# A linear-attention and feed-forward kernel on one core: a step order from priorities replaced by a written-out order

## The chip, the cores and the metric

The kernel runs on one core of one Trainium2 chip. A core has TensorE (PE in the profile; its weight loads are PEld), VectorE (DVE), ScalarE (ACT), GpSimd (POOL), SyncE (SP, which here only issues DMAs) and 16 DMA engines. Each engine works through its own instructions in the order in which the program gave them, and waits at an instruction until what that one needs is there. The metric is the device time of one launch in microseconds (us).

## What is computed

The first half is a linear attention with decay (batch 4, 8 heads, 768 positions, head width 48), the second a feed-forward layer:

```python
for t in range(S):
    cur = np.einsum('bhd,bhe->bhde', u[None] * kt, vt)
    y[:, :, t] = np.einsum('bhd,bhde->bhe', rt, state + cur)
    state = wt[:, :, :, None] * state + np.einsum('bhd,bhe->bhde', kt, vt)
x = y.transpose(0, 2, 1, 3).reshape(B * S, H * D)   # 3072 x 384
h = x @ w_in                                        # 384 x 2048
out = np.maximum(0.01 * h, h) @ w_out               # 2048 x 384
```

All inputs and the output are float32; the matmuls run in bf16.

## The kernel before

**Tiles.** The sequence is cut into 24 chunks of 128 positions (6 per batch). The first two chunks of batches 0 and 1 are done as two pairs (`pair`, chunks 0/1 and 2/3); the others one by one (`single`, chunks 4 to 23, in turn over the batches). Each chunk goes through the same steps:

- SP loads w, k, r and v into a tile `in` (L630 for pairs, L845).
- ACT takes the logarithm of w (L644, L855). TensorE sums it cumulatively with a triangular matrix (L654, L861) and in total (L668, L864). DVE forms `ci` (L873); ACT takes the exponentials (L687, L882, L887, L891).
- DVE multiplies them into r and k (`rk`, L545). Transposing gives `rkT`: by TensorE (L556) with a copy on ACT (L563) or DVE (L561), or, for the chunks in `RK_DMA`, by a transposing DMA (L908).
- POOL casts v (`vb`, L595) and, with a row of `u` spread at the start (L528, L522, L533, L539: `ub`), makes products (`ru`, L575 and L579), which DVE sums (`dg`, L583) and POOL multiplies into v (`vs`, L587).
- TensorE makes the scores (L768, L1002), DVE masks them (`m`, L780, L932). TensorE makes the state's sums (L727, L942), DVE adds the old state (L957), and for the next chunk of the batch POOL scales the state (`sb`, L919; in the pairs DVE, L738).
- TensorE makes y from masked scores, v and state (L793, L800, L812; L968, L973); DVE or ACT takes it out of PSUM (L618; L822, L824). It is transposed into `xT` by TensorE (L604) with a copy (L609, L611), or by a DMA (L987).

**Feed-forward.** The chunks are put together to 15 blocks of one or two. Per block, TensorE makes the up-projection in steps of 512 columns of PSUM (L1168: 6 matmuls of 256 columns, or 12 of 128), ACT applies the leaky ReLU into `g` (L1183), TensorE makes the down-projection in four quarters of four matmuls per chunk (L1198), DVE or ACT copies it (L1209, L1211), SP stores it (L1215). In the last three blocks (`seven`) the down-projection is a scheme with seven products in place of eight (L1098), with sums on DVE (L1048 once for the weights, in `mix`; L1079 for each block; L1119). The weights are loaded at the start in pieces (L466, L471) and cast to bf16 on POOL, DVE or ACT (L488, L490, L492).

**What sets the order.** `Plan` holds 1092 steps. A step has the engines that could do it with a time for each, a function that issues its instructions, a priority, the steps that it depends on, the buffers that it reads and takes, and for a DMA a time on the wire. `Plan.order` (L43) plays this through in time: an engine that comes free takes, of the steps whose inputs are done and whose buffers are free, the one with the lowest priority. `RANK` (L163) shifts the priority of each step by a number, and `FORCE` (L301) ties some steps to one engine. What comes out is the program's order on every engine, and which buffer of its pool each step gets. Limits per kind of PSUM buffer (L450) and a slack (L344) enter too. In the first 24 us of the plan's own time, TensorE gets filler matmuls on zeros (L1240) in its gaps.

A PSUM bank is written and read by several steps, by different engines; the program orders their accesses to one tile in the order in which they are issued.

Of the kernel before, what the change touches and what calls it, by code (L numbers as in the profile page):

```python
# [15 lines left out]
class Buf:  # L16


    def __init__(self, pool, kind=None, wide=1):
        self.wide = wide  # L20
        self.pool, self.kind, self.users, self.t, self.free_at = pool, kind or pool, [], None, 0.0


class Plan:


    ENGINES = ("PE", "DVE", "ACT", "POOL", "SP")
# [4 lines left out]
    def __init__(self, limits, slack_from, slack, late):  # L32
        self.steps, self.limits, self.late = [], limits, late
        self.slack_from, self.slack = slack_from, slack
# [8 lines left out]
    def order(self, pools):  # L43
        n = len(self.steps)
        users = [[] for _ in range(n)]
        left = [len(s[3]) for s in self.steps]
        for i, s in enumerate(self.steps):
            for j in s[3]:
                users[j].append(i)
        bufs = {}  # L50
        for i, s in enumerate(self.steps):
            for b in (*s[4], *s[5]):
                bufs[id(b)] = b
        remain = {k: len(b.users) for k, b in bufs.items()}
        free_tiles = {p: [(0.0, k) for k in range(len(t))] for p, t in pools.items()}
        in_use = {}
        ready_at = [0.0] * n
        self.start, self.done, self.eng = [None] * n, [0.0] * n, [None] * n
        free = dict(self.BEGIN)
        ready = {e: [] for e in self.ENGINES}  # L60
        events = []
        dma_free, flying = 0.0, []

        def offer(i, t):
            for e in self.steps[i][0]:
                heapq.heappush(events, (t, 0, e, i))

        for i in range(n):
            if not left[i]:
                offer(i, 0.0)  # L70
        for e in self.ENGINES:
            heapq.heappush(events, (free[e], 1, e, -1))
        count, out = 0, []
        while events:
            now, kind, e, i = heapq.heappop(events)
            same = {e}
            if kind == 0 and self.start[i] is None:
                heapq.heappush(ready[e], (self.steps[i][2], i))
            elif kind == 2:
                in_use[i] -= 1  # L80
            while events and events[0][0] <= now + 1e-9:
                _, kind, e, i = heapq.heappop(events)
                same.add(e)
                if kind == 0 and self.start[i] is None:
                    heapq.heappush(ready[e], (self.steps[i][2], i))
                elif kind == 2:
                    in_use[i] -= 1
            for e in self.ENGINES:
                if (e not in same and "*" not in same) or free[e] > now + 1e-9:
                    continue  # L90
                held, chosen = [], None
                while ready[e]:
                    pri, i = heapq.heappop(ready[e])
                    if self.start[i] is not None:
                        continue
                    want, ok = {}, True
                    for b in self.steps[i][5]:
                        if b.t is None:
                            want[b.pool] = want.get(b.pool, 0) + 1
                            if in_use.get(b.kind, 0) >= self.limits.get(b.kind, 99):  # L100
                                ok = False
                    for p, k in want.items():
                        if sum(f <= now + 1e-9 for f, _ in free_tiles[p]) < k:
                            ok = False
                    if ok:
                        chosen = i
                        break
                    held.append((pri, i))
                for h in held:
                    heapq.heappush(ready[e], h)  # L110
                if chosen is None:
                    continue
                i = chosen
                engs, fn, pri, deps, reads, takes, wire = self.steps[i]
                for b in takes:
                    if b.t is None:
                        slots = free_tiles[b.pool]
                        s = min(slots)
                        slots.remove(s)
                        b.slot = s[1]  # L120
                        b.t = pools[b.pool][s[1]]
                        in_use[b.kind] = in_use.get(b.kind, 0) + 1
                d = engs[e]
                self.start[i], self.eng[i] = now, e
                out.append(i)
                count += 1
                free[e] = now + d - (self.OVER[e] if d > 0.3 else 0.0)
                if wire is None:
                    self.done[i] = now + d + self.SEEN[e]
                    if self.slack_from <= pri < 1000:  # L130
# [1144 lines left out]
```

## Time and profile before

| | |
|---|---|
| median of 3 runs | 178.79 us (178.79 to 179.43) |
| span of the profiled execution | 177.7 us |
| TensorE busy | 170.7 us, 2106 matmuls |
| DVE, ACT, POOL busy | 133.9, 115.6, 105.3 us |
| DMA moved | 34.24 MB in 115884 packets |

The profiled execution's own time is known by its span alone, from its first to its last instruction; the median of the runs, which also hold what lies around the span, is 1.1 us above it. Busy times of TensorE are modelled: its matmuls overlap, and a busy TensorE is not one at its peak. So what its work costs is read from the chain of waits, which gives for each piece the time from its start to that of the next.

### The profile page before, as it was taken

How to read it: one execution, taken by the hardware profiler on the slowest of the kernel's cores; microseconds unless marked ns; L12 is line 12 of the kernel's file. 1: busy time of each engine (PE TensorE's matmuls, PEld its weight loads, DVE VectorE, ACT ScalarE, POOL GpSimd, SP SyncE). 2: the span in 40 equal slices, each digit the busy share in tenths (PEclk: the TensorE clock that was granted, in tenths of full speed). 3: DMA queues.
4: the chain of work that ended last, by engine and by line, in shares of the span. 5: the costliest groups of instructions: out<-in, count | busy, mean ns of one | idle time of the engine just before them, and what ended most of it. 6: DMA issues, size and time to landing. Idle time of an engine off the chain costs nothing.

```text
span 177.7 us, 5379 instructions
## 1 busy us (share of the span) xinstructions
PE 170.7 (96%) x2106; PEld 133.9 (75%) x2110; DVE 133.9 (75%) x268; ACT 115.6 (65%) x258; POOL 105.3 (59%) x139
## 2 busy tenths in 40 slices
PE   7899899999999999999999999999999999999993
PEld 2456678766879767797788776788777798899992
DVE  7599744568987949979968888699779688776463
ACT  5679877764856687487497891288873677662820
POOL 5998554255897749993905994659884099100000
PEclk9999999999999999999999999999999999999999
DMA  5999999999999999997999999997999996613004
GB/s 142 262 283 341 338 377 325 234 197 168 193 146 210 171 189 191 194 227 171 221 185 209 197 147 222 205 177 155 191 208 148 241 207 160 159 24 111 4 22 157
DMA packets 115884, 34.24 MB, mean 193 GB/s; under 512 B 108305, under 2 KB 115090, under 8 KB 115858
## 3 DMA queue, kind: packets, MB, share of 16 engines
q1 hardware_dynamic: 115856, 33.89, 94.3%
q8 instruction: 16, 0.26, 0.7%
q14 instruction: 10, 0.08, 0.2%
q10 hardware_dynamic: 2, 0.00, 0.0%
HBM read 25.17 MB, written 4.72 MB: 168 GB/s over the span
## 4 chain that ended last, share of the span: by engine, by line
PE 74%; DMA 8%; SPq 5%; ACT 4%; DVE 3%; issue 3%; POOL 1%; DVEq 0%; ACTq 0%; POOLq 0%
PE ps L1168 29%; PE ps L1198 23%; PE ps L1098 8%; DMA in<-in_moe_w_in_dram 5%; SPq L630 4%; DMA in<-in_w_dram 3%; PE ps L1002 3%; PE ps L973 2%; ACT g L1183 2%; PE ps L861 2%; PE ps L556 2%; PE ps L968 2%; PE ps L942 1%; PE ps L604 1%; DVE in L1048 1%
## 5 line engine op out<-in xcount | busy, mean ns | idle before, releaser
L1168 PE MATMUL ps<-xT,w_in_b 128*128 128x256 bf16 (+1 forms) x720 | 73.3, 251 | 0.1
L1183 ACT ACTIVATE g<-ps 128x512 bf16<-128x512 f32 x96 | 55.9, 594 | 22.4 <-PE ps L1168 19.5
L1168 PEld LDWEIGHTS <-w_in_b 128*128 128x128 bf16 x720 | 57.6, 98 | 8.4 <-issue 0.3
L1198 PE MATMUL ps<-w_out_b,g 128*128 128x384 bf16 x288 | 56.5, 326 | 0.0
L1198 PEld LDWEIGHTS <-g 128*128 128x128 bf16 x288 | 25.1, 97 | 12.0
L545 DVE TENSOR_TENSOR rk<-in,ps 128x384 bf16<-128x384 f32 x48 | 25.3, 550 | 8.0 <-ACT ps L887 3.0
L575 POOL TENSOR_TENSOR ru<-in,ub 128x384 f32<-128x384 f32 x24 | 25.4, 1061 | 6.2 <-DMA in<-in_k_dram 6.1
L932 DVE TENSOR_TENSOR m<-ps,maskb 128x512 bf16<-128x512 f32 x40 | 25.3, 682 | 4.2 <-PE ps L1002 3.3
L595 POOL CAST vb<-in 128x384 bf16<-128x384 f32 x24 | 13.2, 553 | 22.3 <-DMA in<-in_v_dram 19.1
L579 POOL TENSOR_TENSOR ru<-ru,in 128x384 f32<-128x384 f32 x24 | 24.4, 1028 | 2.9 <-DMA in<-in_r_dram 2.4
L587 POOL TENSOR_TENSOR vs<-in,dg 128x384 f32<-128x384 f32 x20 | 17.0, 852 | 3.5 <-DVE dg L583 2.9
L919 POOL TENSOR_TENSOR sb<-s,a 128x384 bf16<-128x384 f32 x18 | 14.9, 830 | 3.3 <-ACT a L882 3.3
L873 DVE TENSOR_TENSOR ci<-ps,lw 128x384 f32<-128x384 f32 x20 | 11.1, 553 | 4.5 <-PE ps L861 1.8
L618 DVE TENSOR_TENSOR y<-ps,vs 128x384 bf16<-128x384 f32 x20 | 10.9, 553 | 4.5 <-PE ps L973 4.5
L583 DVE TENSOR_REDUCE dg<-ru 128x8 f32<-128x384 f32 x24 | 13.1, 544 | 0.7 <-POOL ru L579 0.6
L882 ACT ACTIVATE a<-ps 64x4 f32<-64x4 f32 x36 | 6.1, 168 | 11.6 <-DVE ci L873 8.9
L855 ACT ACTIVATE lw<-in 128x384 bf16<-128x384 f32 x20 | 10.1, 520 | 3.8 <-DMA in<-in_w_dram 3.6
L891 ACT ACTIVATE ps<-ci 128x384 f32<-128x384 f32 x20 | 9.7, 485 | 1.8 <-DVE ci L873 1.8
L887 ACT ACTIVATE ps<-ps 128x384 f32<-128x384 f32 x20 | 9.3, 467 | 0.5 <-DVE ci L873 0.3
L1240 PE MATMUL ps<-zeros 128*128 128x128 bf16 (+1 forms) x31 | 7.6, 351 | 1.6 <-DVE zeros L409 1.3
L556 PE MATMUL ps<-ident,rk 128*128 128x128 bf16 x88 | 8.4, 220 | 0.5 <-DVE rk L545 0.4
L1098 PEld LDWEIGHTS <-g 128*128 128x128 bf16 x96 | 8.1, 98 | 0.2
(105 smaller groups left out, 222.5 us busy)
## 6 DMA issues: line engine op xcount, KB each, us to landing
out_dram<-o SPq DMA_DIRECT2D x23, 192.0 KB, 2.7
in<-in_w_dram SPq DMA_DIRECT2D x20, 192.0 KB, 4.6
in<-in_v_dram SPq DMA_DIRECT2D x20, 192.0 KB, 4.9
in<-in_r_dram SPq DMA_DIRECT2D x20, 192.0 KB, 4.4
in<-in_k_dram SPq DMA_DIRECT2D x20, 192.0 KB, 4.6
in<-in_moe_w_out_dram SPq DMA_DIRECT2D x4, 768.0 KB, 8.7
in<-in_moe_w_in_dram SPq DMA_DIRECT2D x4, 384.0 KB, 7.8
in<-in_moe_w_in_dram SPq DMA_DIRECT2D x2, 768.0 KB, 8.5
```

The costliest lines, as they stand in the source:

```text
L545: (nc.gpsimd if e == "POOL" else nc.vector).tensor_tensor(out=o, in0=x, in1=i, op=ALU.mult)
L575: lambda e: nc.gpsimd.tensor_tensor(out=ru.t[:], in0=kv(), in1=ubv, op=ALU.mult),
L579: lambda e: nc.gpsimd.tensor_tensor(out=ru.t[:], in0=ru.t[:], in1=rv(), op=ALU.mult),
L583: lambda e: nc.vector.tensor_reduce(out=dg.t[:], in_=ru.t[:], axis=AX.X, op=ALU.add),
L587: lambda e: nc.gpsimd.tensor_tensor(out=vs.t[:], in0=vv(), in1=dg.t[:].unsqueeze(2).to_broadcast([128, H, D]), op=ALU.mult),
L595: {"POOL": 0.56}, lambda e: nc.gpsimd.tensor_copy(out=vb.t[:], in_=vv()),
L919: lambda e: nc.gpsimd.tensor_tensor(out=sb.t[:].rearrange("p g a d -> p (g a) d"), in0=s_in.t[:].rearrange("p g a d -> p (g a) d"), in1=a_ ...
L932: lambda e, par=par: nc.vector.tensor_tensor(out=m.t[:, par, :, :], in0=sc[par].t[:].rearrange("p (g t) -> p g t", g=NP), in1=maskb[:].uns ...
L1098: nc.tensor.matmul(o(), lhsT=x()[:, i, :], rhs=y()[:, i, :], start=fresh, stop=(stop and i == ii[-1]), skip_group_check=True)
L1168: nc.tensor.matmul(hp.t[:, a * N : (a + 1) * N], lhsT=w_in_b[:, t, (j + a) * 128 : (j + a + 1) * 128], rhs=xT[:, t, c0 : c0 + N], start=(a ...
L1183: lambda e, hp=hp, g=g, j=j, J=J, N=N: nc.scalar.activation(out=g.t[:, j : j + J, 0:N], in_=hp.t[:, 0 : J * N].rearrange("p (a n) -> p a n ...
L1198: nc.tensor.matmul(op.t[:, 0:DM], lhsT=g.t[:, j, off : off + 128], rhs=w_out_b[:, j, :], start=(j == 0), stop=(j == NJ - 1))
```

## The change

The steps and what each computes stay. Changed are:

- `Plan.order` no longer chooses. It goes through a list `ORDER` of all 1092 steps, and gives each engine its steps in that order. A step runs on the engine that `FORCE` names, or on the first one that its `add` call lists. The plan's times are kept, for buffers and for the filler matmuls; a PSUM buffer touched by one engine now counts as in use for the others until that access is done, and DMAs land in order.
- `RANK`, the limits per kind and the slack go. `FORCE` is a new table. By both, 43 steps run on another engine than before: among them the first copy of u's row (L528) from ACT to DVE, y's copies of the first pair (L822, L824) both to ACT and those of the second both to DVE, six of the copies out of transposes (L563) to DVE and five (L561) to ACT, and some weight casts.
- Several step times in the plan are set anew: casts of weights 0.57 on DVE (from 1.0 and 0.66), 0.95 for L1048 (from 1.2), 0.72 for a spaced copy of transposes, 0.68 for masks.
- Buffers: `in` 11 (from 10), `ci` 3 (from 2), `g` 4 (from 3), and the pairs' `rkT2` now takes a `g` buffer. `xT`, one tile for all chunks, becomes six buffers of one block each.
- The filler matmuls end at a step of the list (`warm_end`) as well as at 24 us.

The order itself, where the prediction speaks of it:

- SP, start: w, k, r of the first pair, w of the second, then v of the first (before: v, then w), k and r of the second, weight piece 4, piece 0, v of the second, pieces 1, 3, 2. Before: piece 0 stood ahead of k, and pieces 4 and 2 ahead of v.
- TensorE, first pair: L668 stands behind two of the transposes L556 (before: ahead of all). DVE: L738 behind all four masks L780 (before: between two and two). Up-projection steps of block 0: those of piece 4 first, three of the six ahead of L727 of the second pair, as before.
- SP, later: the w loads of chunks 8, 9, 11 and 13 stand earlier, many v loads later; the v loads of chunks 22 and 23 stand behind their transposing loads L908 (before: ahead).
- TensorE, later: the state sums L942 of chunks 6, 8, 9, 10, 11, 14 and 15 stand later; cumulative sums L861 of most chunks earlier. The last product steps and DVE's last five steps stand as before.
- The four L1048 stand further apart: two together, one, one (before: two together, then one and one with a step or two between).

```diff
     def order(self, pools):
...
+        for i in ORDER:
+            engs, fn, deps, reads, takes, wire = self.steps[i][0], *self.steps[i][1:2], *self.steps[i][3:]
+            if left[i]:
+                raise RuntimeError(("before its inputs", i))
+            e = FORCE.get(i) or next(iter(engs))
+            now = max(at[e], ready[i])
+            for b in takes:
+                if b.t is None:
+                    slot = min(free[b.pool])
+                    free[b.pool].remove(slot)
+                    now, b.slot, b.t = max(now, slot[0]), slot[1], pools[b.pool][slot[1]]
+            touched = list({id(b): b for b in (*reads, *takes)}.values())
+            for b in touched:
+                if b.pool == "ps":
+                    now = max([now, *(t for q, t in b.seen.items() if q != e)])
+            self.start[i], self.eng[i] = now, e
+            at[e] = now + engs[e] - (self.OVER[e] if engs[e] > 0.3 else 0.0)
...
+                landed = self.done[i] = max(wire_free + lat, landed + 0.7 * time)
...
-RANK = {0: -309.63, 1: -310.62, 2: -303.35, 3: -175.12, 4: -176.12, 5: -3.85, 6: -313.07, 7: -303.34, 8:
...
+ORDER = [1090, 0, 1, 2, 3, 4, 5, 6, 7, 11, 14, 12, 13, 20, 18, 19, 21, 8, 25, 26, 27, 36, 22, 23, 40, 24, 15,
...
-    xT = pool.tile([128, KT, NCH * L], BF16, name="xT")
-
-    make("in", 10, [128, 1536], F32)
+
+    make("in", 11, [128, 1536], F32)
...
-    make("ci", 2, [128, H, D], F32)
+    make("ci", 3, [128, H, D], F32)
...
-    make("rkT2", 2, [128, 2 * NP, 256], BF16)
...
-    make("g", 3, [128, NJ, max(blocks) * L], BF16)
+    make("g", 4, [128, NJ, max(blocks) * L], BF16)
+    make("xT", 6, [128, KT, max(blocks) * L], BF16)
...
+        place = {}
+        for nb, size in enumerate(blocks):
+            xb = Buf("xT")
+            for off in range(size):
+                place[len(place)] = (xb, off * L)
...
-            rkT = Buf("rkT2")
+            rkT = Buf("g", "rkT2")
...
-                    {"DVE": 1.2}, sub, MIX_RANK, deps=[*wout_s, last], reads=t[: x // 2 + 1], takes=[t[x // 2]])
+                    {"DVE": 0.95}, sub, MIX_RANK, deps=[*wout_s, last], reads=t[: x // 2 + 1], takes=[t[x // 2]])
```

214 lines of the change are left out of this document (67 added, 147 removed), and 188 rows, old and new, of tables (ORDER, RANK).

## The prediction

> **What bounds the kernel now.** I read the page first: busy shares, the slices and the DMA queue.
>
> ```profile
> span 177.7 us, 5379 instructions
> ...
> PE 170.7 (96%) x2106; PEld 133.9 (75%) x2110; DVE 133.9 (75%) x268; ACT 115.6 (65%) x258; POOL 105.3 (59%) x139
> ...
> PEclk9999999999999999999999999999999999999999
> DMA  5999999999999999997999999997999996613004
> GB/s 142 262 283 341 338 377 325 234 197 168 193 146 210 171 189 191 194 227 171 221 185 209 197 147 222 205 177 155 191 208 148 241 207 160 159 24 111 4 22 157
> DMA packets 115884, 34.24 MB, mean 193 GB/s; under 512 B 108305, under 2 KB 115090, under 8 KB 115858
> ...
> q1 hardware_dynamic: 115856, 33.89, 94.3%
> ```
>
> Two resources are near their limit: TensorE, at full clock in every slice, and the DMA engines, busy until some 150 us (slice 34 of 40). The other three engines have room, so moving a step between DVE, ACT and POOL changes the time only by when its result is there.
>
> Next, the chain of waits (start, us, what), for what TensorE's work costs when nothing holds it up.
>
> ```profile
> 26.05 1.34 PE ps L1168 x24
> 36.13 1.30 PE ps L1198 x8
> 80.96 0.55 PE ps L1002 x16
> 116.20 0.17 PE ps L968 x4
> 116.37 0.20 PE ps L973 x8
> 144.57 3.28 PE ps L1168 x30
> 168.78 5.95 PE ps L1098 x72
> 174.76 0.36 DVE o L1119
> ```
>
> Per step: an up-projection step of a one-chunk block (12 matmuls of 128 columns) takes 0.67, one of a two-chunk block (6 of 256) 3.28/5 = 0.656, a quarter of a down-projection 0.65, an L1098 matmul 0.083. From 26.05 on TensorE has 24 x 0.67 + 66 x 0.656 (all but the first six) + 72 x 0.65 + 168 x 0.083 = 120.1 us of these; scores about 5.8 (seven of 0.55, six near 0.33), the y steps 20 x 0.37 = 7.4, and some 254 small matmuls near 0.05 (transposes, cumulative sums, state sums) 13. That is about 146.5 us. The last matmul ends at 168.78 + 5.95 = 174.7, so the stretch from 26.05 lasts 148.7. **Only about 2.2 us are lost there; the other loss is the first 26 us**, in which TensorE does the two pairs' matmuls and six up steps, an estimated 15 us. A new order can gain in just these two places; behind 174.7 come a 0.36 us addition and a store, 3.0 us, which the change leaves alone.
>
> **The change part by part.** The steps, and the work in each, stay; so does the sum of TensorE's work. New are the order on each engine, the engine of 43 steps, and buffers. I go by stretches of the span.
>
> *The first 26 us.* The timeline there:
>
> ```profile
> 3.18 0.51 ACT L528 COPY o<-o 1x384 f32<-1x384 f32 x1
> 4.84 0.50 PE L533 MATMUL ps<-o,ones_f 128*128 128x384 bf16 x1 [0.20 <-DVE o L522]
> 7.00 1.02 DVE L545 TENSOR_TENSOR rk<-in,ps 128x384 bf16<-128x384 f32 x2 [1.06 <-PE ps L668]
> 11.06 1.29 DVE L780 TENSOR_TENSOR m<-ps,mask 128x512 bf16<-128x512 f32 x2 [0.17 <-PE ps L768]
> 12.27 0.55 DVE L738 TENSOR_TENSOR sb<-ps,a 128x384 bf16<-128x384 f32 x1
> 12.74 1.28 DVE L780 TENSOR_TENSOR m<-ps,mask 128x512 bf16<-128x512 f32 x2
> 14.06 0.57 PE L793 MATMUL ps<-vb,m 64*128 64x48 bf16 x32
> 16.07 0.48 ACT L824 CAST y<-ps 128x384 bf16<-128x384 f32 x1
> 16.10 0.56 DVE L822 CAST y<-ps 128x384 bf16<-128x384 f32 x1 [0.16 <-PE ps L812]
> 18.20 0.81 PE L1168 MATMUL ps<-xT,w_in_b 128*128 128x256 bf16 x6
> 20.68 0.96 POOL L595 CAST vb<-in 128x384 bf16<-128x384 f32 x2 [1.80 <-DMA in<-in_v_dram]
> 21.24 0.22 PE L727 MATMUL ps<-vb,rk 64*128 64x96 bf16 x2 [0.43 <-POOL vb L595]
> ```
>
> - The first row of u (L528, 0.51) goes from ACT to the end of DVE's row of L522, so L533 starts near 5.3 instead of 4.84. The cumulative matmuls waited for the logarithms anyway; I take 0.1 (0 to 0.5). ub, and POOL's chain of products behind it, come 0.3 later, which POOL's row hides until the reductions L583 that stand ahead of the masks on DVE.
> - L668 goes behind two transposes. DVE's first product waited 1.06 and named L668; without it it can start near 6.6 instead of 7.00: -0.4.
> - L738 goes behind all four masks instead of between them: the last mask, and with it L793, come up to 0.55 earlier, near 13.45 instead of 14.06.
> - The pair's two L824 copies and the two xT copies now all stand on ACT, with an L563 copy between them, where before ACT and DVE shared them (16.07 and 16.10). That is 2 x 0.48 on the path, and the 0.6 gained is given back: the first up-projection starts near 18.5 instead of 18.20, +0.3.
> - SP now issues the second w ahead of the first v, and one 384 KB weight load that stood ahead of the second pair's v goes behind it. At the page's 338 GB/s in that slice, 393 KB is an estimated 1.2 us: v, for which POOL waited 1.80, comes near 19.5, and L727 starts behind three up-projections near 20.6 instead of waiting up to 21.24. What follows up to the first step of block 1 is the same list of steps.
>
> Together the row at 26.05 moves to about 25.2: **-0.9**, from -1.6 (v 1.8 earlier and no series on ACT) to +0.8 (ACT's series costs its full length, v is no earlier).
>
> *From there to the last chunks.* The two largest stalls, by the chain, and the DVE rows beside the second:
>
> ```profile
> 55.41 6.14 DMA in<-in_w_dram
> 61.57 0.52 ACT lw L855
> ...
> 66.35 0.33 PE ps L942 x4
> ...
> 127.88 0.42 ACT lw L855
> ...
> 128.35 0.32 PE ps L861
> ```
>
> ```profile
> L1048 DVE TENSOR_TENSOR in<-w_out_b x2: 1236/1494/1751, 118.2 to 119.3; 128x1536 bf16<-128x1536 bf16 x2
> ```
>
> ```profile
> 159.59 0.69 DVE L1079 TENSOR_TENSOR in<-g 128x1024 bf16<-128x1024 bf16 x1 [0.73 <-ACT g L1183]
> ```
>
> The first is a late w load: the logarithm, the sums and the exponentials behind it end in L942, for which TensorE waits half a microsecond. In the new order the w loads of chunks 8 and 9 stand five and nine places earlier in SP's row and that L942 step 22 places later in TensorE's, so this wait goes. The second is ACT's logarithm at 127.88, behind products that DVE did late because of four subtractions L1048. They ran beside POOL steps and took 1.24 to 1.75; L1079, of the same kind and with POOL at rest, took 0.69 for 1024 columns, so 1536 should take near 1.03. Spread out and kept apart from POOL, the four give back up to 4 x 0.45 = 1.8 us of DVE. What is late next: the state sums L942 of five chunks go 17 to 28 us later in TensorE's work, and the state update, POOL's scaling and the next chunk's y now follow with little between (the one of chunk 6 has some 2.2 us of TensorE steps before chunk 10's y, for a path of 0.17 + 0.55 + 0.83 and the hand-overs). I take half of the loss, **-1.1**, from -2.2 (all of it) to +2 (several new waits of half a microsecond).
>
> [...]
>
> *Buffers.* An eleventh load buffer lets SP run ahead of the chunks; a third ci, a fourth g and six xT blocks remove waits that no row shows to be on the chain: 0. The shared g and rkT2 cost nothing as long as the pairs are done before the fourth block, which the order has.
>
> *The end.* The last products and DVE's last five steps stand as before: 0.
>
> **How the DMA limits this.** SP's rows and chunk 22, the last one computed:
>
> ```profile
> in<-in_v_dram SPq DMA_DIRECT2D x20, 192.0 KB, 4.9
> ```
>
> ```profile
> 141.92 2.08 SPq L845 DMA_DIRECT2D in<-in_v_dram  x2
> 147.27 0.50 POOL L595 CAST vb<-in 128x384 bf16<-128x384 f32 x1
> 147.69 0.33 PE L861 MATMUL ps<-lw,trev 128*128 128x384 bf16 x1
> 151.13 1.29 SPq L908 DMA_TRANSPOSE rkT<-rk  x1
> 157.73 0.33 PE L968 MATMUL ps<-sb,rkT 128*128 128x96 bf16 x4
> ```
>
> Behind the start of chunk 22's y (157.73) the new order leaves TensorE ten up steps, 136 L1098 matmuls and the y itself: 6.6 + 11.3 + 0.4 = 18.2 us; before, 17.0 passed to the end. So to end by 172.7, 2 us earlier, that y must come at 154.5. Its k and r loads keep their places. The transposing load at 151.13 waited for a cumulative sum that came late in TensorE's row (147.69) and now stands twelve places earlier there. Issued by 148, with both v loads now behind it (1.3 for itself, about 1.5 for what follows, 3 to 4.9 to land), v is there at 153.8 to 155.7 and y half a microsecond later. This is about the -2 of the sum, and it is why I don't take the whole -3.1.
>
> **The sum.** 177.7 - 0.9 - 1.1 = 175.7 of span. The profile gives no more of its own execution than the span; the median of the runs, 178.79, lies 1.1 above it, which I carry over: **176.8 us**.
>
> **Rivals.**
>
> *The DMA sets the pace all the same.* For: 94.3% and nines in every slice to 150; the bytes stay; chunks' y steps stand 1 to 6 us earlier in TensorE's work than they ran, so TensorE may merely wait for them. Against: only y's of late loads matter, and stores and far-ahead loads were moved behind. Then 157.73 stays and the time is 178.3 to 179.4. [...]
>
> *A head-of-line wait in SP's queue: slower.* Chunk 22's and 23's v loads were issued at 141.92; now they stand behind the transposing loads of both chunks, and those behind DVE's products. If the last of these is issued no earlier than before (151.13), v is issued near 153.9 and lands at 156.9 to 158.8, and y comes at 157.6 to 159.5 with 18.2 behind it: 1 to 3 us later than now, 179.9 to 181.8. It decides from an issue at about 149.5 on.
>
> *The new order doesn't do what it says:* the first 26 us get longer by 0.8 and the new state waits eat the rest: 178.8 to 180.
>
> **How the numbers follow.** A measurement of this kernel tells about 0.5% from no change: 177.9 to 179.7 is "the same". Forecast 0.55 (175.2 to 177.9), the whole gain and more 0.07 (under 175.2), the DMA's pace 0.16, SP's queue 0.12, the order itself 0.10, half of it slower. So faster 0.62, same 0.21, slower 0.17. The range 175.0 to 180.3 leaves out about 0.05 below and 0.1 above.
>
> **What would show it.** Right: the first step of block 1 near 25.2; L727 without a wait for vb; L1048 near 1.0; no L942 on the chain at 66; chunk 22's y at 153.5 to 156; the last matmul near 172.7. Wrong: transposing loads of chunks 22 and 23 issued after 149.5, POOL's cast of v waiting just ahead of the last y, a first up-projection past 19, or TensorE idle in the middle slices with ACT or DVE named. The prediction fails in its sum if the first 26 us don't shorten, since more than half of the rest rests on waits that I only know in the old order.

## The result and the profile after

The changed kernel takes 180.02 us (median of 20 runs, 178.91 to 181.97), the kernel before 179.23 (20 runs, 178.77 to 179.57). The ratio is **1.0032 [1.0019, 1.0045]**: a third of a per cent slower. In a later set of runs it was 1.0046 [1.0022, 1.0071]. One of the changed kernel's 20 executions in the first set (181.97, at a granted clock of 0.991) fell into a slower state and is left out of the ratio. The profiled execution took 180.19; its span is 178.5, 0.8 longer than before, and the forecast was 175.7.

The changed kernel's code is shorter, so that the same step has a line number some 140 lower: the up-projection L1168 is L1028 now, the down-projection L1198 is L1058, the cumulative sum L861 is L722, the logarithm L855 is L716, the scores L1002 are L862, the loads L845 are L706. In the experiments the numbers differ a little again.

The page of the changed kernel, the lines that answer to those shown of before:

```profile
span 178.5 us, 5374 instructions
...
PE 169.7 (95%) x2103; PEld 133.9 (75%) x2106; DVE 132.6 (74%) x275; ACT 111.9 (63%) x249; POOL 105.1 (59%) x141
...
PEclk9999999999999999999999999999999999999999
DMA  5999999998999999999999999996998938721113
...
q1 hardware_dynamic: 115856, 33.89, 94.8%
q8 instruction: 16, 0.26, 0.6%
```

Work, clock and bytes are those of before; what changed is waiting. So I compare the two traces step by step: for each TensorE step the time from its start to the next one's, above what steps of its kind take at their shortest. Three differences make up the span.

**The first 26 us: -1.1, as forecast.** The timeline of the changed kernel (start, us, engine, line, operation; in brackets the wait ahead of it):

```profile
5.32 0.34 PE L393 MATMUL ps<-o,ones_f 128*128 128x384 bf16 x1 [0.47 <-DVE o L388]
...
6.65 1.95 DVE L405 TENSOR_TENSOR rk<-in,ps 128x384 bf16<-128x384 f32 x4 [0.39 <-ACT ps L549]
...
18.08 2.21 PE L1028 MATMUL ps<-xT,w_in_b 128*128 128x256 bf16 x18
...
20.45 0.52 PE L589 MATMUL ps<-vb,rk 64*128 64x96 bf16 x16 [0.16 <-POOL vb L455]
```

```profile
24.11 3.05 PE L1028 MATMUL ps<-xT,w_in_b 128*128 128x256 bf16 x46
```

In the last row six matmuls (0.66) end block 0, so block 1 starts at 24.77. Before, it started at 25.89 by the same timeline; the chain, which counts from the modelled end of the matmul ahead, put that row at 26.05.

**The middle: +1.5.** The old stalls at 66.35 and 127.88 are gone. The list of TensorE's waits (us in total, times, longest) names a new one, and the chain (start, us, what) shows where it comes from:

```profile
PE ps L722 <- ACT lw L716: 1.8, 1, 1.8
...
PE ps L862 <- DMA rkT<-rk: 0.4, 1, 0.4
```

```profile
34.32 7.66 DMA in<-in_w_dram
42.00 0.53 ACT lw L716
42.57 0.32 PE ps L722
...
47.59 5.72 DMA rkT<-rk
53.36 0.62 PE ps L862 x16
```

The w load of chunk 6, issued at 34.32, lands 7.66 us later; ACT takes the logarithm, and TensorE sums it at 42.57. TensorE's timeline there:

```profile
40.44 0.36 PE L834 MATMUL ps<-vb,m 128*128 128x48 bf16 x8
42.57 0.32 PE L722 MATMUL ps<-lw,trev 128*128 128x384 bf16 x1 [1.77 <-ACT lw L716]
```

By the step-by-step comparison it has then waited 1.92 us; the row says 1.77, since it counts from the modelled end of the matmul ahead. (The other waits of TensorE below are given by the comparison too, and their rows say up to 0.2 less.) Ten us later the scores of the same chunk wait 0.58 for their transposing load. Over all steps from 26 us on the waits add up to 2.7 us before and 4.2 after: the two new ones cost 2.5, and all others together fell from 2.7 to 1.7. Behind 53 no wait of this size follows.

**The end: +0.4.** The last matmul ends at 175.13 (174.72 before), and the span ends 3.35 behind it instead of 2.99. The stores are not what takes longer: the last one lands 2.06 behind the last matmul (2.07 before). SyncE takes note of that landing at 2.08 in both. Its next step begins at 2.15 before and at 2.46 in the changed kernel, though what that step asks for had been there before the last matmul ended. This goes with the program: the end takes 3.35 and 3.34 in the two profiles of the changed kernel, and 3.33 to 3.35 with w of chunk 6 two loads earlier, with 24 matmuls more, with less filler, and in the old order listed (3.48 with the old counts of buffers). It takes 2.97 to 3.00 in the eleven others: the kernel before and its variants, the new front with the old order, and all versions in which w of chunk 6 goes ahead of the weight pieces. What sets it is not shown. It is part of every execution's time, so that 0.35 us, or 0.2%, of a difference between these two groups has nothing to do with loads.

-1.1 + 1.5 + 0.4 = +0.8, from 177.7 to 178.5.

Why was w of chunk 6 late? SP's row in the changed kernel, and below it the same stretch before:

```profile
29.72 1.29 SPq L321 DMA_DIRECT2D in<-in_moe_w_out_dram  x2
31.07 0.56 SPq L706 DMA_DIRECT2D in<-in_v_dram  x1
31.67 2.60 SPq L706 DMA_DIRECT2D in<-in_k_dram  x1
34.32 3.40 SPq L706 DMA_DIRECT2D in<-in_w_dram  x1
37.77 0.88 SPq L706 DMA_DIRECT2D in<-in_r_dram  x1
```

```profile
21.04 6.40 SPq L471 DMA_DIRECT2D in<-in_moe_w_out_dram  x2
...
30.65 3.42 SPq L845 DMA_DIRECT2D in<-in_k_dram  x1
34.11 1.38 SPq L845 DMA_DIRECT2D in<-in_w_dram  x2
```

and ACT's row of before, in which the logarithm of chunk 6 waits for nothing:

```profile
39.48 0.54 ACT L855 ACTIVATE lw<-in 128x384 bf16<-128x384 f32 x1
```

The load is issued at about the same time in both (the second of the two at 34.11). But the last two weight pieces (768 KB each, L321), issued from 21.04 on before, now stand at 29.72, just ahead of it, and it queues behind them: it lands at 41.98, before by 39.48 at the latest. At the same time the new order asks for it earlier. Before, the cumulative sum of chunk 6 ran at 44.50:

```profile
44.50 0.33 PE L861 MATMUL ps<-lw,trev 128*128 128x384 bf16 x1
```

Now it stands right behind y of chunk 4, which ends at 40.80. A slack of four us became a lack of nearly two.

### The profile page after: what moved, and what is told of

Its sections match the earlier page's. It is cut to its first block, busy times and chain, and to the rows that moved or that the text cites. A ratio compares the mean times of both kernels' runs of the same rounds, so it can differ in the third digit from the quotient of the medians.

```text
span 178.5 us, 5374 instructions
## 1 busy us (share of the span) xinstructions
PE 169.7 (95%) x2103; PEld 133.9 (75%) x2106; DVE 132.6 (74%) x275; ACT 111.9 (63%) x249; POOL 105.1 (59%) x141
## 4 chain that ended last, share of the span: by engine, by line
PE 75%; DMA 12%; SPq 7%; ACT 2%; issue 1%; DVE 1%; POOL 1%; DVEq 0%; POOLq 0%
PE ps L1028 33%; PE ps L1058 20%; PE ps L958 8%; DMA in<-in_moe_w_in_dram 4%; DMA in<-in_w_dram 4%; SPq L492 4%; DMA rkT<-rk 3%; PE ps L862 3%; PE ps L834 2%; SPq L706 2%; PE ps L829 2%; PE ps L722 2%; PE ps L466 1%; PE ps L803 1%; PE ps L416 1%
## 5 line engine op out<-in xcount | busy, mean ns | idle before, releaser
L1028 PE MATMUL ps<-xT,w_in_b 128*128 128x256 bf16 (+1 forms) x720 | 71.4, 252 | 0.2
L1028 PEld LDWEIGHTS <-w_in_b 128*128 128x128 bf16 x720 | 57.5, 98 | 7.8 <-issue 0.7
L1058 PE MATMUL ps<-w_out_b,g 128*128 128x384 bf16 x288 | 54.5, 326 | 0.0
L1058 PEld LDWEIGHTS <-g 128*128 128x128 bf16 x288 | 26.1, 97 | 13.5 <-ACT g L1043 0.2
L405 DVE TENSOR_TENSOR rk<-in,ps 128x384 bf16<-128x384 f32 x48 | 24.7, 550 | 7.2 <-ACT ps L748 3.0
L435 POOL TENSOR_TENSOR ru<-in,ub 128x384 f32<-128x384 f32 x24 | 24.4, 1022 | 4.4 <-DMA in<-in_k_dram 3.2
L780 POOL TENSOR_TENSOR sb<-s,a 128x384 bf16<-128x384 f32 x18 | 14.7, 828 | 16.0 <-DVE s L818 11.0
L455 POOL CAST vb<-in 128x384 bf16<-128x384 f32 x24 | 12.0, 504 | 14.5 <-DMA in<-in_v_dram 10.3
L447 POOL TENSOR_TENSOR vs<-in,dg 128x384 f32<-128x384 f32 x20 | 16.5, 829 | 1.9 <-DMA in<-in_k_dram 1.4
L716 ACT ACTIVATE lw<-in 128x384 bf16<-128x384 f32 x20 | 10.0, 524 | 3.0 <-DMA in<-in_w_dram 3.0
L338 POOL CAST w_out_b<-in 128x768 bf16<-128x768 f32 x5 | 4.9, 981 | 7.4 <-DMA in<-in_moe_w_out_dram 7.4
L818 DVE TENSOR_TENSOR s<-ps,sb 128x384 f32<-128x384 f32 x14 | 7.6, 551 | 2.1 <-POOL vs L447 0.7
L1071 ACT COPY o<-ps 128x384 f32<-128x384 f32 x11 | 5.3, 479 | 6.1 <-PE ps L1058 6.0
```

Source lines behind the costliest of these rows:

```text
L405: (nc.gpsimd if e == "POOL" else nc.vector).tensor_tensor(out=o, in0=x, in1=i, op=ALU.mult)
L435: lambda e: nc.gpsimd.tensor_tensor(out=ru.t[:], in0=kv(), in1=ubv, op=ALU.mult),
L447: lambda e: nc.gpsimd.tensor_tensor(out=vs.t[:], in0=vv(), in1=dg.t[:].unsqueeze(2).to_broadcast([128, H, D]), op=ALU.mult),
L455: {"POOL": 0.56}, lambda e: nc.gpsimd.tensor_copy(out=vb.t[:], in_=vv()),
L780: lambda e: nc.gpsimd.tensor_tensor(out=sb.t[:].rearrange("p g a d -> p (g a) d"), in0=s_in.t[:].rearrange("p g a d -> p (g a) d"), in1=a_ ...
L1028: nc.tensor.matmul(hp.t[:, a * N : (a + 1) * N], lhsT=w_in_b[:, t, (j + a) * 128 : (j + a + 1) * 128], rhs=xb.t[:, t, 0:N], start=(a == 0 ...
```

## The experiments

The runs were made in five sets, each beside the kernel before, whose median lay between 179.06 and 179.44; the ratio is to that of the same set, and between sets only ratios can be compared. Each median is of 4 to 12 executions, and each trace is of one of them.

| run | median, us | ratio |
|---|---|---|
| old order listed, new code and buffers | 180.08 | 1.0046 [1.0029, 1.0064] |
| new front, then old order | 179.44 | 0.9997 [0.9980, 1.0014] |
| w of chunk 6 two loads earlier | 179.84 | 1.0026 [1.0004, 1.0048] |
| w of chunk 6 ahead of both weight pieces | 179.53 | 1.0006 [0.9986, 1.0026] |
| old order, old PSUM buffers | 181.12 | 1.0087 [1.0066, 1.0109] |
| old order, old counts of buffers | 181.49 | 1.0094 [1.0068, 1.0121] |
| before, 24 matmuls more at 26 us | 180.49 | 1.0059 [1.0040, 1.0078] |
| changed, 24 matmuls more at 26 us | 180.16 | 1.0048 [1.0028, 1.0067] |
| old order, old filler | 179.33 | 1.0013 [0.9998, 1.0029] |
| before, more filler | 179.51 | 1.0024 [1.0000, 1.0047] |
| changed, less filler | 179.66 | 1.0031 [1.0014, 1.0047] |
| w of 6 ahead of both, less filler | 179.31 | 1.0017 [0.9992, 1.0042] |
| before, matmuls split | 184.45 | 1.0296 [1.0265, 1.0327] |
| new front, k of 15 earlier | 178.87 | 0.9994 [0.9979, 1.0010] |
| the same, w of 4 earlier | 179.18 | 1.0009 [0.9995, 1.0023] |
| w of 6 and transposing load of 6 earlier | 178.46 | 0.9984 [0.9958, 1.0010] |
| the same, one cast later | 178.73 | 0.9990 [0.9962, 1.0017] |
| the changed kernel again | 179.95 | 1.0046 [1.0022, 1.0071] |

My theory after the two traces: the front's gain is real and is lost at one late load. Rivals: the order behind the front is worse as a whole; the buffers cost something; the loads' pace as a whole takes back whatever TensorE gains.

**Old order, new everything else.** The list is that of before (and its engines); code and buffers are the new ones.

```diff
-ORDER = [1090, 0, 1, 2, 3, 4, 5, 6, 7, 11, 14, 12, 13, 20, 18, 19, 21, 8, 25, 26, 27, 36, 22, 23, 40, 24, 15,
+ORDER = [0, 7, 1090, 1, 8, 9, 2, 4, 10, 3, 5, 11, 63, 6,
...
```

> The order and engines of the kernel before, written out as a list in the changed kernel, with its buffers (11 load buffers, six xT blocks, the pairs' rkT2 in g). If buffers and the way of giving the order cost or bring nothing (theory), 178.8 to 179.5, the same within 0.5%, and the first step of block 1 near 25.9. If the shared g and rkT2 or the xT blocks bring waits of their own (rival), 1 us or more above that, with a wait on TensorE between 25 and 60 us that the kernel before doesn't have.

It took 1.0046 where I had expected 1: something besides the order cost 0.8 us. Its trace has a wait of 0.72 at 73 us, behind the r load of chunk 11 (landed 71.88, before 71.11), 0.36 at 82 to 84, and the longer end (3.33). I come back to it.

**New front alone.** The new list up to block 1's first step (747), then the rest in the old order.

> The changed order up to the first step of block 1, then the order of the kernel before, with its DMA order from there. Theory (the first 26 us gain 1.1 us, and one late w load behind them takes it away): the first step of block 1 near 24.8, no wait of over 0.5 us on TensorE between 26 and 60 us, and 1.0 us less than the kernel before (0.994). Rival (the rest is paced by the DMA, so an earlier start is waited away): TensorE reaches block 1 early and then waits for loads, and the time is that of the kernel before within 0.3%.

Block 1 starts at 24.55, and yet the time is that of before. Two places show where most of the gain went: TensorE waits 0.47 at 30.4 us for the logarithm of chunk 4's w, and 0.78 at 100 us. The timeline of DVE and of TensorE:

```profile
100.12 0.55 DVE L397 TENSOR_TENSOR rk<-in,ps 128x384 bf16<-128x384 f32 x1 [1.09 <-DMA in<-in_k_dram]
```

```profile
30.40 0.32 PE L714 MATMUL ps<-lw,trev 128*128 128x384 bf16 x1 [0.30 <-ACT lw L708]
...
100.73 0.34 PE L795 MATMUL ps<-vb,rk 128*128 128x96 bf16 x4 [0.64 <-DVE rk L397]
```

The k load of chunk 15 landed at 100.02 (99.71 before): TensorE came early, waited, and went on at the old time (100.73; the same step ran at 100.64 before). What is gained at the front is lost at loads that have no slack.

**w of chunk 6 earlier**, in two places (203 is that load, 148 the v load of chunk 4, 139 the first of the two weight pieces):

```diff
-... 166, 167, 148, 150 ...
+... 166, 167, 203, 148, 150 ...
```

```diff
-... 731, 732, 139, 141 ...
+... 731, 732, 203, 139, 141 ...
```

> The changed kernel with one step moved: SP issues the w load of chunk 6 two loads earlier, ahead of chunk 4's v and chunk 5's k. Theory (one wait at 40.4 us, of 1.9 us, for this load): the load lands near 40, the wait is under 0.5 us, and the time falls by 1 to 1.8 us against the changed kernel, to 0.993 to 0.998 of the kernel before. Rival (the DMA's backlog is late as a whole, so another load is late in its place): the wait moves to chunk 4's y or to the scores of chunk 6, and the time stays near 1.003.

> The changed kernel with the w load of chunk 6 issued ahead of the last two weight pieces too. Theory: the load lands near 35, no wait for it; what is late next is the weight pieces, 1.1 us later than now, and the v and k loads behind them, so 0.993 to 1.000. Rival (the backlog as a whole is late): a wait on TensorE for weights or for chunk 4's y of 1 us or more, and 1.003 or more.

Two loads earlier, w landed at 39.41, and a wait of 1.25 came up a little later: DVE stood before the k load of chunk 5, which had gone behind w, and y of chunk 4 behind that on DVE. Its timelines:

```profile
41.90 0.55 DVE L399 TENSOR_TENSOR rk<-in,ps 128x384 bf16<-128x384 f32 x1 [2.25 <-DMA in<-in_k_dram]
```

```profile
43.44 0.34 PE L460 MATMUL ps<-ident,y 128*128 128x128 bf16 x3 [1.09 <-DVE y L474]
```

Ahead of both weight pieces it landed at 33.70 and the wait was gone; what came in its place were 0.39 ahead of the transposing of chunk 4's y and 0.32 ahead of the scores of chunk 6. That trace is of the fastest of its twelve executions (178.48; the median is 179.53). The ratio fell from 1.0032 to 1.0006, about 0.5 us, and 0.35 of that is the end (3.00 instead of 3.35). So the place in SP's row is what made w late, as the landings show; but that taking away this one wait wins back its 1.9 us at the median is not shown, and the front's gain did not come out.

**More work ahead of the wait.** Two up-projection steps of block 1 do their matmuls twice, 1.34 us more for TensorE near 26 us, in the kernel before and in the changed one:

```diff
-                    for a in range(J):
+                    for a in [*range(J)] * (2 if nb == 1 and j in (0, 8) else 1):
```

> The kernel before, in which the first and the third up-projection step of block 1 (near 26 us) run their 12 matmuls twice: 24 matmuls or about 1.34 us more work for TensorE at that place, with the same results. If TensorE's own row sets the end from 26 us on, as the prediction's sum takes it, the time rises by the whole 1.3, to 180.6 to 180.8 (ratio 1.0075). If the loads set the pace later on (the gain of 1.1 to 2.0 us at the front was gone by 100.7 us in the run with the new front alone, where a step waited 0.78 for a product behind the k load of chunk 15), a loss at 26 us is caught up in part: under 180.1, ratio under 1.004.

> The changed kernel with the same 24 matmuls more in block 1's first and third up-projection step. If the late w load of chunk 6 (landed 41.98, a wait of 1.92 on TensorE) swallows what the front gained, it swallows this too: the wait at 42 falls to some 0.6 and the time stays within 0.3 of 180.0 (ratio to before 1.002 to 1.005). If front and wait add up, 181.2 to 181.5 (ratio 1.010 or more).

Before pays 1.06 of the 1.34, between the two forecasts (0.7 to 1.4 by the interval): there TensorE's own row does set the time, with little slack. The changed kernel pays about 0.3 (1.0048 against 1.0032, no more than the noise), and its wait for the logarithm has shrunk from 1.8 to

```profile
PE ps L716 <- ACT lw L710: 0.3, 1, 0.3
```

Up to 42 us the loads set its pace. A front that is 1.1 faster is worth nothing there, and one that is slower costs almost nothing.

**What makes a load late.** The old order listed was still to be explained. Two guesses fell: with before's PSUM buffers pinned, and with the old counts of buffers, it got no faster.

```diff
-                    slot = min(free[b.pool])
+                    slot = min(s for s in free[b.pool] if want is None or s[1] == want)
```

> The order of before in the new kernel's code and with its larger buffers, as in the old order listed, but every step is given the PSUM buffer that it had before. The old order listed took 180.08 (1.0046 of before), and 247 of its 352 PSUM buffers were other ones than before, since the code's model of the time chooses them. Theory: the 0.8 us come from PSUM buffers that are not yet free when their step comes (0.36 us ahead of a down-projection at 82.6 in that trace): near 179.4, ratio within 0.9985 and 1.002, and no wait ahead of the down-projections at 81 to 83. Rival: they come from the other buffers (an eleventh load buffer, the shared g, the split xT) or from the loads' landing: 180.1 again, ratio 1.003 or more.

```diff
-    make("in", 11, [128, 1536], F32)
+    make("in", 10, [128, 1536], F32)
...
-    make("g", 4, [128, NJ, max(blocks) * L], BF16)
+    make("g", 3, [128, NJ, max(blocks) * L], BF16)
```

> The order of before in the new code, with the old counts of buffers (10 load buffers, 2 ci, 3 g, a pool of its own for the pairs' transposed tiles) and an xT buffer for every block, but with the new code's choice of PSUM buffers. Theory that PSUM buffers cost the 0.8 us: 180.1 again, ratio 1.003 or more. Rival, the load buffers and the shared pool cost them: near 179.4, ratio within 0.9985 and 1.002. The prediction put the buffers at 0.

Both waited at the same two places, 73 and 82 to 85 us, and took 0.4 to 0.5% more than the first listing, which stays unexplained. But the traces side by side showed something else. In each, the DMA engines run nearly empty for about half a microsecond, at most places some 10.7 us apart. DMA share and GB/s of the kernel before from 38 to 43 us, in 40 slices of 0.125 us:

```profile
DMA  9999999999999999999999863224699999944578
GB/s 247 258 237 220 177 286 134 151 184 192 192 192 177 181 154 155 154 175 181 217 212 164 148 97 60 40 46 84 117 178 229 261 252 229 178 82 88 91 120 163
```

and of the changed kernel:

```profile
DMA  9666999999867879999954310000148999997567
GB/s 140 94 83 111 200 189 174 229 368 211 146 111 124 135 147 183 218 206 206 163 100 77 52 15 11 17 15 15 25 97 180 207 233 241 255 227 152 103 124 129
```

The spikes (286 at 38.7, 368 at 39.0) are one packet of 16384 bytes in the queue that the page calls q8 instruction. There are 16 of them for TensorE's 4209 matmuls and weight loads. Some 2 us behind each of the two the other loads run dry: a dip in the first row, a hole of 0.7 us in the second, just ahead of w's landing. The ten extra filler matmuls of the listed order (45 instead of 35, since the code fills the gaps of its own plan) should shift these packets by 20 instructions: near 70 us one came at 69.2 to 69.7 in the three listed runs and at 70.0 before. So I gave the listed order the filler of before, and before that of the listed order:

```diff
-                    for n in (512, 128):
-                        while gap > n * per:
...
+                    for n in FILL.get(i, ()):
```

> The old order listed in the new code, as in the first experiment (180.08, ratio 1.0046), but with the 35 warming matmuls of the kernel before at their places instead of the 45 that the new code's model of the time puts into the first 21 us. The traces show a packet of 16384 bytes in the queue named q8 instruction after every 256 or so matmuls and weight loads of TensorE, SP held for about 2.3 us from that moment, and the DMA engines nearly empty some 2.25 us later (share 0.1 to 0.5 for half a microsecond). Theory: which load this delays is a matter of phase, and ten more warming matmuls move it by 20 instructions, 0.8 us, onto the r load of chunk 11 (landed 71.88 to 72.51 in three such runs, 71.11 before): with the old count the time is near 179.4, ratio within 0.9985 and 1.002. Rival: the buffers or the listing cost the 0.4 to 0.9%: ratio 1.003 or more.

> The kernel before, with nothing changed but its warming matmuls: 45 at the places of the old order listed, instead of 35. All of them stand in gaps of the first 21 us. Theory of the phase: the packets of instructions come 0.8 us earlier, r of chunk 11 lands near 72 and the step behind it waits 0.5 to 1: ratio 1.003 to 1.009. Rival: filler in gaps costs nothing, ratio within 0.9985 and 1.002.

With the old filler the listed order is at 1.0013, most of the 0.8 us gone; r of chunk 11 landed at 70.61, and no wait for it is left. The longer end (3.34) alone would make 1.002, so buffers and listing cost nothing else that can be told. The converse, 1.0024, points the same way, but its interval touches 1 and its one trace, of the fastest of its twelve executions, has no wait for chunk 11; that direction is not shown. Nor is it shown that the filler acts through the packets and not otherwise. Less filler in the changed kernel (one word, `for n in (512,)`):

> The changed kernel with warming matmuls of 512 columns only: 17 instead of 31, so 28 instructions fewer on TensorE ahead of 17 us. Theory of the phase: the packet of instructions at 39.01 comes at about 40.2, the DMA engines run empty at 42.4 instead of 40.9, the w load of chunk 6 lands near 41.0 instead of 41.98, and the wait of 1.92 at 42 falls to about 1: ratio 0.996 to 1.000, if no other load is hit instead. Rival, the w load is late by its place in SP's row alone: the wait stays at 1.9, ratio 1.002 to 1.005.

> The changed kernel with the w load of chunk 6 ahead of the last two weight loads, as in the run with it earlier (179.53, ratio 1.0006), and with warming matmuls of 512 columns only. There w of chunk 6 was already early (33.70), so the theory of the phase promises nothing at 42; the packets of instructions move by 1.2 us everywhere and may hit other loads: ratio 0.995 to 1.004. A candidate for a kernel faster than both.

In the profiled execution, again the fastest of its twelve, w landed at about 40.5 and the wait was 0.62. But w had been issued a us earlier (33.33 instead of 34.32), the packet had not moved (38.76), and the median is that of the changed kernel. So the forecast of the phase failed here. With w of chunk 6 early as well, 1.0017 is no better than 1.0006 without. The filler is no lever.

That the packets make the dips is tested by changing their spacing: the kernel before, its matmuls split.

```diff
-                                rhs=xT[:, t, c0 : c0 + N], start=(a == 0 and t == 0),
+                                    rhs=xT[:, t, c0 + h : c0 + h + 128], start=(a == 0 and t == 0 and h == 0),
```

> The kernel before with every up-projection matmul of 256 columns split into two of 128 and every down-projection matmul of 384 columns split into three of 128, each with its own weight load: the same arithmetic in some 970 matmuls more, 1940 instructions more on TensorE. Up steps of that shape take 0.67 instead of 0.656 and three times 0.055 is what a matmul of 384 takes, so TensorE's own work rises by 1 to 2 us. Theory: TensorE's instructions come through the same DMA engines, 16384 bytes after every 256, and each such packet empties the DMA engines for half a microsecond about 2 us later. Then some 23 packets instead of 16 stand in q8, one every 7.5 us instead of 10.7, the low slices of the DMA move with them to that spacing, and the loads fall behind: 182 to 186 us. Rival: the low slices every 10.7 us belong to something else (the loads' own pattern, refresh): they stay where they are, and the time is 180 to 181.

The page now counts more packets, the engine's spike stands at 40.1, and the hole is 2 us behind it, where before had none:

```profile
q8 instruction: 24, 0.39, 1.0%
```

```profile
DMA  9999999999999999999999999999999620000378
GB/s 237 232 238 244 253 240 206 175 154 169 198 172 189 209 197 201 322 195 204 197 189 187 183 188 181 175 183 194 195 197 172 83 25 11 14 14 17 65 144 172
```

24 packets for 6232 matmuls and weight loads, one every 7 us, and the holes went with them. The rival, a pattern of the loads themselves, is out. (Of the 5.3 us, TensorE's busy time accounts for 3.2; what the rest is can't be told apart.)

**Single loads or the pace as a whole?** With the new front, k of chunk 15 (468) moved ahead of w of chunk 16 (504), and then also w of chunk 4 (145) ahead of a weight piece (136):

```diff
-... 869, 440, 504, 471 ...
+... 869, 440, 468, 504, 471 ...
```

```diff
-... 130, 136, 145, 139 ...
+... 130, 145, 136, 139 ...
```

> The new front with the old order behind it (179.44 against 179.37, ratio 0.9997), with one load moved: the k load of chunk 15, for which a step waited 0.78 at 100 us, goes three loads ahead in SP's row (ahead of w of chunk 16). If what the front gains is lost at this one load, it lands near 97, the wait goes and the time falls by 0.8: 178.5, ratio 0.994 to 0.997. If the loads as a whole set the pace, the next load takes its place and the time stays: ratio 0.998 to 1.001.

> As the run before it, and the w load of chunk 4, ahead of which TensorE waited 0.47 at 29.3, goes ahead of the 768 KB weight load before it. If single loads are what is lost: another 0.3 to 0.4 less than the run before it. If the loads as a whole set the pace: the same time, or later, since the weight load lands 0.6 later.

The wait at 100 went and the time stayed (0.9994): smaller waits elsewhere took its place. With w of chunk 4 earlier too, its wait went, the weight piece that it had passed came late instead, TensorE waited 1.02 for that at 31.5 us, and the time stayed again (1.0009). With the new order, the same game went better: the transposing load of chunk 6 (217) ahead of w of chunk 9 (295), then a weight cast (141) behind two copies on DVE:

```diff
-... 198, 245, 295, 784 ...
+... 198, 245, 217, 295, 784 ...
```

```diff
-... 159, 160, 180, 181 ...
+... 159, 160, 180, 141, 181 ...
```

> The changed kernel with the w load of chunk 6 ahead of the last two weight loads (179.53, ratio 1.0006), and the transposing load of chunk 6, behind which its scores waited 0.32 (0.58 in the changed kernel), ahead of the w load of chunk 9. Single waits theory: 0.3 less, ratio 0.997 to 1.001. Pace of the loads as a whole: no change, 0.9995 to 1.003.

> The version of the run before (w of chunk 6 and the transposing load of chunk 6 earlier; 178.46, ratio 0.9984), in which DVE waited 1.63 for a weight piece and chunk 4's two copies of transposed tiles stood behind that cast: TensorE waited 0.38 for them at 37.96. Now the cast stands behind the two copies on DVE. Single waits theory: 0.4 less, ratio 0.994 to 0.999. Pace of the loads as a whole: the wait moves on to the next load and the ratio stays within 0.997 and 1.001.

> The changed kernel once more, on the same chip as the version with its three waits taken out, for a second profile of it and for a direct comparison. The wait of 1.92 at 42 was there in one profile; if the late w load of chunk 6 is what holds the changed kernel in most executions, it is between 0.6 and 2 again, and the ratio 1.002 to 1.005.

The changed kernel again waited for chunk 6's w, and in the version with the three edits the last matmul of the profiled execution, one of the faster ones (178.12), ends at 173.39 instead of 174.88. The changed kernel's timeline in this second profile:

```profile
42.45 0.32 PE L722 MATMUL ps<-lw,trev 128*128 128x384 bf16 x1 [1.56 <-ACT lw L716]
```

Run together, 178.73 against 179.95, the three edits are worth 0.6% or 1.2 us. Of that 0.35 is the end (3.00 against 3.34), so that some 0.9 came from the waits. So for the new order the theory of single waits holds in part: it gives back about 0.9 of the 1.5 us that its middle had lost. Against before, 0.9984 and 0.9990 with 1 inside both intervals: not shown to be faster. Their runs fall into two groups (178.1 to 178.8 and 179.4 to 180.3); I take it for which loads the packets hit, but only one execution of each was profiled, so this stays open.

## Why the prediction was wrong, point by point

**What bounds the kernel: right in its numbers, wrong in what follows from them.** Work of some 146 us from 26 us on fits both traces, and the 2.2 lost there are 2.7 by the comparison of steps. But 24 more matmuls cost 1.06 of 1.34 before, and a front 1.1 faster brought nothing: a loss is paid, a gain is not. TensorE's row and the loads were both without slack, and the sum treated only TensorE's.

**The first 26 us: right**, -1.1 for -0.9. L528 on DVE put u's matmul L533 at 5.32 (near 5.3 forecast), DVE's first product started at 6.65 (6.6), L727's step at 20.45 without a wait worth the name (20.6). The first up-projection came at 18.08: ACT's series of copies did not cost the 0.3 that stood for it (18.5).

**The middle: this step failed.** It said that the stalls at 66 and 127.88 go, and they did: the old waits fell by 1.0, close to the -1.1 that it took. For what comes instead it allowed up to +2, as "several new waits of half a microsecond", and put nothing into the sum. It came as one wait of 1.92 and one of 0.58, 2.5 in all and +1.5 with the gain. The step had read SP's new row for chunks 8, 9, 22 and 23 and not for chunk 6, whose w now stood close behind two weight pieces that before had been issued 9 us and more ahead of it, while its sum moved four us ahead in TensorE's row. For the late state sums, where I had looked for the danger, TensorE waited nowhere.

**L1048: half right.** The timeline of the changed kernel, DVE and POOL:

```profile
115.98 2.62 DVE L908 TENSOR_TENSOR in<-w_out_b 128x1536 bf16<-128x1536 bf16 x2
121.48 1.28 DVE L908 TENSOR_TENSOR in<-w_out_b,in 128x1536 bf16<-128x1536 bf16 x1
126.14 0.95 DVE L908 TENSOR_TENSOR in<-w_out_b,in 128x1536 bf16<-128x1536 bf16 x1
```

```profile
116.23 1.56 POOL L435 TENSOR_TENSOR ru<-in,ub 128x384 f32<-128x384 f32 x1 [1.80 <-DMA in<-in_k_dram]
...
121.44 0.50 POOL L455 CAST vb<-in 128x384 bf16<-128x384 f32 x1
```

Alone the step takes 0.95 (1.03 estimated). Three of the four still met POOL: at 121.48 one took 0.33 more beside a cast of 0.50, and the pair at 116 took 2.62 together beside a product that itself took 1.56 instead of 1.00. At 116 both engines are slowed; at 121.48 the 0.33 lost is less than the cast's whole 0.50. What makes them slow each other is not shown. None of it reached TensorE.

**Buffers at 0: right** as far as can be told (1.0013 [0.9998, 1.0029] with the filler held, longer end included). What I had not seen is that the list also changes the filler.

**The end at 0: wrong by 0.4.** The products, the addition and the store do stand as before; what grew is SyncE's last steps, behind the store's landing, and why is open.

**The DMA's limit on chunk 22: mechanism right, size by what came before it.** The end of the changed kernel's timeline, SP and TensorE:

```profile
147.31 2.63 SPq L769 DMA_TRANSPOSE rkT<-rk  x2
150.03 0.53 SPq L706 DMA_DIRECT2D in<-in_v_dram  x1
...
151.28 0.42 SPq L706 DMA_DIRECT2D in<-in_v_dram  x1
```

```profile
156.82 0.33 PE L829 MATMUL ps<-sb,rkT 128*128 128x96 bf16 x4
```

Chunk 22's transposing load was issued at 147.31 (by 148 in the forecast), chunk 23's at 148.66, and v was there in time; y stands at 156.82 without a wait, and 18.3 us of TensorE follow it (18.2 forecast). It came 2.3 later than the 154.5 because TensorE was late itself. The rival of SP's queue is refuted by the same rows: it had v issued near 153.9.

**The sum.** The 1.1 between span and time was mis-sized: it is 1.7 in every run that has both (180.19 against 178.5), since the profiled execution of before was not the median one. Of the 3.2 us by which 176.8 missed the median of 180.02, that is 0.6; the middle is 2.6 (+1.5 for -1.1), the end 0.4, the front -0.2, and the profiled execution lies 0.2 above the median.

**The rivals.** "The DMA sets the pace all the same" came nearest, at another place than it said: not at chunk 22's y, which did move, but at chunk 6's w, and in the run with the new front alone at chunk 4's w and chunk 15's k. Its price was wrong, though: with y left at 157.73 and the 18.2 us of the new order behind it, the last matmul ends at 175.9, which makes 180.0 by the prediction's own sum and not 178.3 to 179.4.

## What to carry to other kernels

Where two resources are both full, as here, a gain on one can be worth nothing until the other's queue is re-read: for every load that the change moves or that it moves something ahead of, set its new landing against the new place of the step that needs it, not only for the loads at the end. Ask of a faster stretch which load it will be early for. And when a rewritten schedule also changes filler or instruction counts, hold those fixed in the control, or the control measures them. Look at the end of the trace as well, behind the last useful instruction: here 0.35 us of a difference of 0.8 stood there.

## What the runs showed of the hardware

The queue that the page calls q8 instruction moves packets of 16384 bytes, on the same 16 DMA engines as the data by the page (0.6% of their span in the changed kernel), and their number goes with TensorE's instructions: 16 for 4209 matmuls and weight loads, 24 for 6232, one for about 260. What I had not expected is their price for the data: over 164 such packets in twenty traces (35 to 118 us) the loads move some 200 GB/s in the two microseconds ahead of the packet and 103 in the half microsecond that begins 2.0 behind it, 143 and 154 in those beside it. SP's DMA issue that spans the packet lasts 2.0 at the median; the one that spans a moment far from any packet lasts 0.9. That is roughly half a microsecond of loading lost per packet, an estimate from these rates, 8 times in this stretch. That the load which a packet delays depends on how many instructions TensorE has behind it is my assumption: the one attempt to move a packet by that (28 instructions fewer) left it where it was (38.76 us for 39.01).
